# Windowed attention and a token and channel mixer on one core: the 64-row matmuls of token mixing replaced by 128-row ones

## The chip, the cores and the metric

The kernel runs on one core of a Trainium2 chip. A core has a matmul engine (PE; its weight loads are shown apart as PEld), a vector engine (DVE), an activation engine (ACT), a general engine (POOL) and a queue engine (SP) that issues transfers. Each takes its own instructions in order; they wait for each other through semaphores. The metric is the device time of one execution in microseconds, as the median of several runs; lower is better.

## The reference

Attention with a causal window of 64 positions over q, k, v of 8 batches, 8 heads, 576 positions and 64 elements per head; then a mixer over the 576 positions (tokens) and one over the 512 channels, each with a residual:

```python
scores = np.where((rel >= 0) & (rel < 64), q @ k.T / 8, -1e9)
x = softmax(scores) @ v                          # (8, 576, 512), heads side by side
h = relu(x.transpose(0, 2, 1) @ w_tok1) @ w_tok2 # w_tok1 576 x 256, w_tok2 256 x 576
u = x + h.transpose(0, 2, 1)
out = u + relu(u @ w_ch1) @ w_ch2                # w_ch1 512 x 1536, w_ch2 1536 x 512
```

All tensors are float32; the weights arrive as float64 and are converted on the chip.

## The kernel before, in words

The 576 positions of a batch are nine blocks of 64. A tile of 128 rows holds two blocks. Two batches (a pair) make nine tiles: four of the one batch, then a shared tile (`i % 9 == 4`) with the ninth block of the first batch in its top 64 rows and that of the second in its bottom 64 rows, then four of the other batch. There are 36 tiles, and one iteration of the main loop (lines 451 to 523) for each, in a software pipeline. In iteration `i` PE computes the scores of tile `i + 1` (`qk`, L257), transposes the first half of tile `i`'s exponentials (L292, copied out of PSUM by ACT at L294), runs a first piece of token mixing (line 486), transposes the second half, runs the first token product of tile `i - 1` (`tok1`, L348), multiplies the probabilities of tile `i` with v (`av`, L304) and runs a second piece (line 510). DVE masks the scores and takes their maximum (L274, L277), ACT takes the exponentials (L285), DVE normalizes (L318), ACT and POOL split the result into a rounded and a remainder part, xhi and xlo (L91, L94; for the shared tile L329 and L330). Between these DVE converts the float64 weights (L179 to L194), with the last addition on POOL (L196).

Products that need full precision are made of three: high by high, high by low, low by high. For the shared tile `split_x` puts the high part of one batch's block and its low part on top of each other in 128 rows (xhi for the first batch, xlo for the second), and the weights' rows of the ninth block are held twice, so that one 128-row matmul with t1hi makes two of the three products. The third, with t1lo, takes the 64 rows of the high part alone:

```python
x = xhi if rows is top else xlo
combos = ((t1hi, x, full), (t1lo, x, rows))
```

`tok1_part` is called four times with 64 rows in each pair's two iterations after the shared tile: two token halves for the first batch (top), two for the second (bottom), so 16 such matmuls in all.

A piece of token mixing (`tok2`) is one batch, one half of its positions and one group of 128 channels: it transposes x into PSUM (L383), adds six matmuls with the second token weights (L390), and ACT copies the result to u (L395). A piece of the first half has two transposes and 256 columns; one of the second half has a third transpose of 64 columns, from 64 rows of the shared tile, and 320 columns. There are 32 pieces of either kind. A table of counts (`PIECES`) sets how many run where: mostly one at line 486 and one at line 510, with the last ones after the loop.

The order of the instructions on each engine is that of the program. From line 572 on, the channel mixing runs on chunks of 512 tokens (L582, L618).

Of the kernel before, what the change touches and what calls it, by code (L numbers as in the profile page):

```python
# [10 lines left out]
F32 = mybir.dt.float32  # L11
F32R = mybir.dt.float32r
# [10 lines left out]
P = 128  # L23
BLK = 64
NBLK = S // BLK
NPAIR = B // 2
TPP = 9
NT = NPAIR * TPP
DT = 256
# [45 lines left out]
def mixer_kernel(ctx: ExitStack, tc: tile.TileContext, qh, kh, vh, wt1, wt2, wc1, wc2, out):  # L75
    nc = tc.nc
# [6 lines left out]
    ident = const.tile([P, P], F32, name="ident")  # L83
# [5 lines left out]
    def split(eng_hi, eng_lo, hi, lo, src):  # L89
        if eng_hi is nc.scalar:  # L90
            nc.scalar.copy(hi, src)  # L91
        else:
            eng_hi.tensor_copy(hi, src)
        eng_lo.tensor_sub(lo, src, hi.bitcast(F32))  # L94
# [18 lines left out]
    with ExitStack() as actx:  # L113
        pa = actx.enter_context(tc.tile_pool(name="pa", bufs=1))
# [24 lines left out]

        maskr = [pa.tile([P, P], F32R, name=f"maskr{m}") for m in range(2)]  # L140
        identr = pa.tile([P, P], F32R, name="identr")
        make_identity(nc, ident)
        nc.scalar.copy(identr, ident)
        for m in (1, 0):
            nc.gpsimd.memset(mask[m], 0.0)
            for half in range(2):
                mh = mask[m][half * BLK:(half + 1) * BLK]
                nc.gpsimd.affine_select(out=mh, in_=mh, compare_op=ALU.is_ge, fill=NEG,
                                        base=-1, pattern=[[1, P]], channel_multiplier=-1)
                nc.gpsimd.affine_select(out=mh, in_=mh, compare_op=ALU.is_ge, fill=NEG,  # L150
                                        base=BLK, pattern=[[-1, P]], channel_multiplier=1)
            if m == 1:
                nc.gpsimd.memset(mask[1][0:BLK, 0:BLK], NEG)
            nc.scalar.activation(maskr[m], mask[m], AF.Copy, scale=NEG_PE / NEG)

        t1hi = pa.tile([P, 5 * DT], F32R, name="t1hi")
        t1lo = pa.tile([P, 5 * DT], F32R, name="t1lo")
        t2hi = pa.tile([P, NTT * S], F32R, name="t2hi")
# [69 lines left out]
        def job_finish():  # L228
            if to_finish:
                n, w = to_finish.pop(0)  # L230
                finished.add(n)
                src, hi, lo, o, m = jobs[n]
                if hi is None:
                    nc.sync.dma_start(w2_dram[:, o:o + m], w)
                else:
                    eng = nc.vector if src is wt2 or n >= N_FIRST else nc.gpsimd
                    split(nc.scalar, eng, hi[:, o:o + m], lo[:, o:o + m], w)

        s_ps, e_sb, st = {}, {}, {}

# [56 lines left out]
        xs, xhl = {}, {}  # L297
# [23 lines left out]
        full, top, bottom = slice(0, P), slice(0, BLK), slice(BLK, P)  # L321
# [13 lines left out]
        h_ps = {}  # L335

        def tok1_part(i, b, rows, slot, first, last):
            xhi, xlo = xhl[i]
            if first:
                h_ps[b] = [ps.tile([P, C], F32, name=f"h{b}_{tt}", tag="h") for tt in range(NTT)]  # L340
            for tt in range(NTT):
                if rows is full:
                    combos = ((t1hi, xhi, full), (t1hi, xlo, full), (t1lo, xhi, full))
                else:
                    x = xhi if rows is top else xlo
                    combos = ((t1hi, x, full), (t1lo, x, rows))
                for n, (w, x, r) in enumerate(combos):
                    nc.tensor.matmul(h_ps[b][tt], w[r, slot * DT + tt * P:slot * DT + (tt + 1) * P], x[r],  # L348
                                     start=first and n == 0, stop=last and n == len(combos) - 1)

        pieces, up_tags = [], [("up", 1)]
# [18 lines left out]
        def tok2(b, half, ct, hh):  # L370
            assert len(finished) >= 7
            p, odd = divmod(b, 2)
            base = p * TPP + (5 if odd else 0)
            s0, n = (0, 256) if half == 0 else (256, 320)
            up = ps.tile([P, 512], F32, name=f"up{b}_{half}_{ct}", tag=up_tags[0][0], bufs=up_tags[0][1])
            up_tags.append(up_tags.pop(0))
            cs = slice(ct * P, (ct + 1) * P)
            segs = [(base + 2 * half + j, slice(0, P), j * P, P) for j in range(2)]
            if half == 1:
                r = slice(BLK, P) if odd else slice(0, BLK)  # L380
                segs.append((p * TPP + 4, r, 256, BLK))
            for j, (i, rows, o, m) in enumerate(segs):
                nc.tensor.matmul(up[:, o:o + m], xs[i][rows, cs], ident[rows, rows],  # L383
                                 start=(j == 0), stop=False, is_transpose=True, skip_group_check=True)
            k = 0
            for tt in range(NTT):
                hi, lo = hh[tt]
                for hx, w in ((hi, t2hi), (hi, t2lo), (lo, t2hi)):
                    k += 1
                    nc.tensor.matmul(up[:, :n], hx[:, cs], w[:, tt * S + s0:tt * S + s0 + n],  # L390
                                     start=False, stop=(k == 6), skip_group_check=True)
            if ct == 0:
                ust[b, half] = pa.tile([P, NCT, 320], F32, name=f"u{b}_{half}", tag="ust", bufs=2)
            us = ust[b, half]
            nc.scalar.copy(us[:, ct, :n], up[:, :n])  # L395
            if ct == NCT - 1:
                stores.append((us, b * S + s0, n))
                if b >= B - 2:
                    store_u()
# [3 lines left out]
        def store_u():  # L403
            while stores:
                us, g0, n = stores.pop(0)
                a = 0
                while a < n:
                    j, o = divmod(g0 + a, CHUNK)
                    m = min(n - a, CHUNK - o)
                    (nc.sync if g0 < (B - 1) * S - 320 else nc.scalar).dma_start(u_dram[j][:, :, o:o + m], us[:, :, a:a + m])  # L410
                    a += m

        def tok1(i):
            p, t = divmod(i, TPP)
            b0, b1 = 2 * p, 2 * p + 1
            if t < 4:
                tok1_part(i, b0, full, t, t == 0, False)
            elif t == 4:
                tok1_part(i, b0, top, 4, False, True)
                finish_h(b0)  # L420
            else:
                if t == 5:
                    tok1_part(i - 1, b1, bottom, 4, True, False)
                tok1_part(i, b1, full, t - 5, False, t == 8)
                if t == 8:
                    finish_h(b1)

        def run_pieces(k):
            for _ in range(min(k, len(pieces))):
                tok2(*pieces.pop(0))  # L430
# [15 lines left out]
        tok1_plan, n = {}, 0  # L446
        for i in range(TOK1_FROM, NT + 1):
            m = min(n + (1 if i < TOK1_SLOW else 2), i)
            tok1_plan[i] = range(n, m)
            n = m  # L450
        for i in range(-1, NT + 1):
# [26 lines left out]
            while to_finish:  # L478
                job_finish()
# [36 lines left out]
            if i == NT - 1:  # L516
                while to_convert or to_convert_b or to_finish:
                    job_convert_a()
                    job_convert_b()
                    job_finish()  # L520
                qctx.close()
                pu = uctx.enter_context(tc.tile_pool(name="pu", bufs=1, side="right", reuse_waits="tile"))
                ul = {0: load_u(0, pu)}
# [4 lines left out]
    with ExitStack() as bctx:  # L528
# [28 lines left out]
        def late_steps():  # L557

            job_abs()
            yield  # L560
            while to_convert or to_convert_b or to_finish:
                job_convert_a()
                if to_load:
                    job_load()
                yield
                job_finish()
                yield
                job_convert_b()
                job_abs()
                yield  # L570
# [89 lines left out]
```

## Time and profile before

| | |
|---|---|
| median of 3 runs | 886.76 us (886.35 to 886.89) |
| the profiled execution's own time | 888.41 us |
| its span in the profile | 886.5 us |
| PE busy | 864.6 us of the span |
| DVE, ACT, POOL busy | 372.3, 311.8, 101.4 us |
| token mixing and attention | to about 294 us, channel mixing from there |

PE is nearly always busy in the records, but the records of its matmuls overlap: what a matmul costs is read from the start of one to the start of the next. A row of the timeline gives the start, the duration, the engine, the line, and the operation with its output, inputs and shape, and, in square brackets, idle time ahead of it with the engine that ended it. Rows of the chain of work give start, duration, engine, output and line. Rows of groups give the count after the x, then the busy time in all and the mean duration in nanoseconds, then the idle time ahead. Rows of stretches of time give for each engine busy time and count, in the order PE, PEld, DVE, ACT, POOL, and then the granted PE clock as a share of full speed.

### The profile page before, as it was taken

What the parts mean: (1) busy time and instruction counts of PE and PEld (TensorE: products, weight loads), DVE (VectorE), ACT (ScalarE), POOL (GpSimd) and SP (SyncE); (2) the same over time, 40 slices, a digit from 0 to 9 for tenths busy, and PEclk for the clock granted to TensorE, in tenths of its full rate; (3) what the DMA queues carried; (4) which work ended last, traced back from release to release, by engine and by line L of the source; (5) the groups of instructions that cost most, each with busy time, mean ns of one, the idle gap of its engine ahead of it and who ended that gap; (6) DMA issues with size and microseconds to landing.
All of it is one profiled execution on the core that took longest, in us unless ns stands there. A gap on an engine that the chain in (4) does not pass through costs nothing.

```text
span 886.5 us, 14562 instructions
## 1 busy us (share of the span) xinstructions
PE 864.6 (98%) x6002; PEld 708.6 (80%) x6002; DVE 372.3 (42%) x701; ACT 311.8 (35%) x966; POOL 101.4 (11%) x104
## 2 busy tenths in 40 slices
PE   7899999999999999999999999999999999999998
PEld 4667878778768888888888888888888888888887
DVE  4978777787776598130220220230220220220211
ACT  4878778778776452120120120120120220220200
POOL 2433343333332000000000000000000000000000
PEclk9989999999999999999999999999999999999999
DMA  9557566566554442100100100100100100100001
GB/s 324 188 180 248 180 229 229 196 204 225 199 175 132 130 156 90 59 1 36 60 0 36 60 1 36 60 1 36 60 12 24 60 13 24 60 13 36 0 13 36
DMA packets 39906, 84.69 MB, mean 96 GB/s; under 512 B 5280, under 2 KB 18336, under 8 KB 37920
## 3 DMA queue, kind: packets, MB, share of 16 engines
q1 hardware_dynamic: 37728, 81.93, 27.5%
q10 hardware_dynamic: 2112, 1.84, 0.6%
q8 instruction: 47, 0.77, 0.4%
q14 instruction: 19, 0.16, 0.1%
HBM read 64.09 MB, written 19.66 MB: 94 GB/s over the span
## 4 chain that ended last, share of the span: by engine, by line
PE 84%; DVE 9%; ACT 4%; issue 1%; DMA 1%; SPq 0%; POOL 0%; DVEq 0%; ACTq 0%
PE op L618 33%; PE gp L582 31%; PE up L390 5%; PE xp L304 4%; PE s L257 4%; PE h L348 3%; PE up L383 2%; ACT e L285 2%; PE pp L292 2%; DVE nm L277 1%; DVE e L274 1%; ACT pt L294 1%; DMA k<-kh 1%; DVE r L194 1%; DVE c L191 1%
## 5 line engine op out<-in xcount | busy, mean ns | idle before, releaser
L586 ACT ACTIVATE ghi<-gp 128x512 fp32r<-128x512 f32 x108 | 64.6, 598 | 440.3 <-PE gp L582 439.9
L618 PE MATMUL op<-ghi,w2lo 128*128 128x512 f32 (+1 forms) x444 | 170.3, 384 | 0.2 <-DVE w2lo L94 0.2
L618 PE MATMUL op<-ghi,w2hi 128*128 128x512 f32 (+1 forms) x444 | 170.2, 383 | 0.0
L618 PE MATMUL op<-glo,w2hi 128*128 128x512 f32 (+1 forms) x444 | 170.2, 383 | 0.0
L582 PE MATMUL gp<-uhi,w1hi 128*128 128x512 f32 x432 | 168.1, 389 | 0.0
L582 PE MATMUL gp<-ulo,w1hi 128*128 128x512 f32 x432 | 168.1, 389 | 0.0
L582 PE MATMUL gp<-uhi,w1lo 128*128 128x512 f32 x432 | 168.1, 389 | 0.0
L587 DVE SCALAR_TENSOR_TENSOR glo<-gp,ghi 128x512 fp32r<-128x512 f32 x108 | 74.6, 691 | 190.6 <-ACT ghi L586 190.6
L620 DVE TENSOR_TENSOR uf<-op,uf 128x512 f32<-128x512 f32 (+1 forms) x37 | 25.0, 677 | 242.1 <-PE op L618 242.1
L618 PEld LDWEIGHTS op<-ghi,w2lo 128*128 128x128 f32 x444 | 83.5, 188 | 17.0 <-DVE w2lo L94 0.6
L618 PEld LDWEIGHTS op<-glo,w2hi 128*128 128x128 f32 x444 | 83.5, 188 | 16.4
L618 PEld LDWEIGHTS op<-ghi,w2hi 128*128 128x128 f32 x444 | 83.5, 188 | 16.3
L285 ACT ACTIVATE e<-e,nm 128x128 f32<-128x128 f32 x232 | 90.4, 393 | 13.9 <-DVE nm L277 11.4
L582 PEld LDWEIGHTS gp<-uhi,w1lo 128*128 128x128 f32 x432 | 81.1, 188 | 16.9
L582 PEld LDWEIGHTS gp<-ulo,w1hi 128*128 128x128 f32 x432 | 81.1, 188 | 16.8
L582 PEld LDWEIGHTS gp<-uhi,w1hi 128*128 128x128 f32 x432 | 81.1, 188 | 16.8
L304 PEld LDWEIGHTS xp<-v,pt 128*64 128x64 f32 x1152 | 41.0, 143 | 21.6 <-ACT pt L294 9.5
L304 PE MATMUL xp<-v,pt 128*64 128x64 f32 x1152 | 48.7, 234 | 6.4 <-ACT pt L294 6.0
L274 DVE SCALAR_TENSOR_TENSOR e<-s,mask 128x512 f32<-128x512 f32 x58 | 39.5, 680 | 26.7 <-PE s L257 26.7
L294 ACT COPY pt<-pp 128x512 f32<-128x512 f32 x72 | 41.7, 584 | 22.1 <-PE pp L292 21.7
L94 POOL TENSOR_TENSOR xlo<-x,xhi 128x512 fp32r<-128x512 f32 x32 | 41.2, 1287 | 55.5 <-ACT xhi L91 55.3
L257 PE MATMUL s<-k,q 64*64 64x128 f32 x1152 | 45.8, 295 | 1.4 <-DMA k<-kh 0.7
(72 smaller groups left out, 1000.0 us busy)
## 6 DMA issues: line engine op xcount, KB each, us to landing
v<-vh SPq DMA_DIRECT2D x36, 512.0 KB, 3.7
raw<-wc SPq DMA_DIRECT2D x32, 384.0 KB, 4.4
q<-qh SPq DMA_DIRECT2D x36, 256.0 KB, 4.1
k<-kh SPq DMA_DIRECT2D x7, 1280.0 KB, 7.8
out<-uf SPq DMA_DIRECT2D x35, 256.0 KB, 2.3
uf<-u_dram SPq DMA_DIRECT2D x8, 1024.0 KB, 5.8
u_dram<-u SPq DMA_DIRECT2D x7, 512.0 KB, 4.5
k<-kh SPq DMA_DIRECT2D x5, 256.0 KB, 7.0
```

Source lines behind the costliest of these rows:

```text
L94: eng_lo.tensor_sub(lo, src, hi.bitcast(F32))
L257: nc.tensor.matmul(s[u][half * BLK:(half + 1) * BLK, j], qt[r, j, half], kbs[b][r, j, n * BLK:n * BLK + P], start=not on_pe, stop=True, sk ...
L274: nc.vector.scalar_tensor_tensor(out=e, in0=s_ps.pop((i, u)), scalar=scale, in1=mk.unsqueeze(1).to_broadcast([P, 4, P]), op0=ALU.mult, op1 ...
L285: nc.scalar.activation(e[:, h], src[:, h], AF.Exp, bias=nm[:, g:g + 1], scale=by, accum_out=sm[:, g:g + 1])
L294: nc.scalar.copy(pt, pp)
L304: nc.tensor.matmul(xp[half * BLK:(half + 1) * BLK, h], pts[h % 2][:, h // 2, half * BLK:(half + 1) * BLK], vt[:, half, h], start=True, sto ...
L348: nc.tensor.matmul(h_ps[b][tt], w[r, slot * DT + tt * P:slot * DT + (tt + 1) * P], x[r], start=first and n == 0, stop=last and n == len(co ...
L390: nc.tensor.matmul(up[:, :n], hx[:, cs], w[:, tt * S + s0:tt * S + s0 + n], start=False, stop=(k == 6), skip_group_check=True)
L582: nc.tensor.matmul(gp, w[:, ct * F + ft * P:ct * F + (ft + 1) * P], x[:, ct], start=(k == 0), stop=(k == 3 * NCT - 1))
L586: nc.scalar.activation(ghi, gp, AF.Relu)
L587: nc.vector.scalar_tensor_tensor(out=glo, in0=gp, scalar=0.0, in1=ghi.bitcast(F32), op0=ALU.max, op1=ALU.subtract)
L618: nc.tensor.matmul(op, w[:, ct, ft], x[:, cols], start=(k == 0), stop=(k == 3 * NFT - 1))
```

## The change

Two kinds of 64-row work on PE become 128-row work, with zeros or a permutation in place of the narrower operand. For the third product of the shared tile a new tile `t1z` holds the low weights of the ninth block twice: once with the top 64 rows and zeros below, once with the bottom 64 rows and zeros above. POOL clears it at the start and copies the rows in when the last part of t1lo is done. For the third transpose the whole 128 rows of the shared tile are transposed, to 128 columns of PSUM of which 64 are used; for the second batch of a pair the identity has its two column halves swapped (`swapped`, made by two copies on POOL), so that the wanted block lands first. The two new tiles take 2.5 KB of each partition.

```diff
+        swapped = pa.tile([P, P], F32, name="swapped")
         make_identity(nc, ident)
...
+        for c in range(2):
+            nc.gpsimd.tensor_copy(swapped[:, c * BLK:(c + 1) * BLK], ident[:, (1 - c) * BLK:(2 - c) * BLK])
+
+        t1z = pa.tile([P, 2, DT], F32R, name="t1z")
+        nc.gpsimd.memset(t1z.bitcast(F32), 0.0)
...
                     split(nc.scalar, eng, hi[:, o:o + m], lo[:, o:o + m], w)
+                    if src is wt1 and o + m == 5 * DT:
+                        for c, r in enumerate((top, bottom)):
+                            nc.gpsimd.tensor_copy(t1z[r, c], t1lo[r, 4 * DT:].bitcast(F32))
...
-                    combos = ((t1hi, x, full), (t1lo, x, rows))
-                for n, (w, x, r) in enumerate(combos):
-                    nc.tensor.matmul(h_ps[b][tt], w[r, slot * DT + tt * P:slot * DT + (tt + 1) * P], x[r],
+                    combos = ((t1hi, x), (None, x))
+                for n, (w, x) in enumerate(combos):
+                    w, o = (t1z[:, rows is bottom], 0) if w is None else (w, slot * DT)
+                    nc.tensor.matmul(h_ps[b][tt], w[:, o + tt * P:o + (tt + 1) * P], x,
...
-            segs = [(base + 2 * half + j, slice(0, P), j * P, P) for j in range(2)]
+            segs = [(base + 2 * half + j, ident, j * P) for j in range(2)]
             if half == 1:
-                r = slice(BLK, P) if odd else slice(0, BLK)
-                segs.append((p * TPP + 4, r, 256, BLK))
-            for j, (i, rows, o, m) in enumerate(segs):
-                nc.tensor.matmul(up[:, o:o + m], xs[i][rows, cs], ident[rows, rows],
+
+                segs.append((p * TPP + 4, swapped if odd else ident, 256))
+            for j, (i, perm, o) in enumerate(segs):
+                nc.tensor.matmul(up[:, o:o + P], xs[i][:, cs], perm,
```

On PE, a piece of the second half of batch 1, the second of a pair, reads before like this; the shapes are those of the output, and the numbers behind the names tell buffers apart:

```order
L383 MATMUL up_1_0_1643<-ident,x_998 128x128
L383 MATMUL up_1_0_1643<-ident,x_1116 128x128
L383 MATMUL up_1_0_1643<-ident,x_689 128x64
L390 MATMUL up_1_0_1643<-t2hi,hhi_0_1208 128x320
L390 MATMUL up_1_0_1643<-t2lo,hhi_0_1208 128x320
```

And now:

```order
L393 MATMUL up_1_0_1650<-ident,x_1005 128x128
L393 MATMUL up_1_0_1650<-ident,x_1123 128x128
L393 MATMUL up_1_0_1650<-swapped,x_696 128x128
L400 MATMUL up_1_0_1650<-t2hi,hhi_0_1215 128x320
L400 MATMUL up_1_0_1650<-t2lo,hhi_0_1215 128x320
```

Nothing moved; the third transpose reads all rows of the shared tile against the swapped identity and writes 128 columns in place of 64.

On PE, the shared tile's first token product for batch 0, between the transposes of the exponentials and the attention product, before:

```order
L292 MATMUL pp_1_750<-ident,e_1_647 128x128 x4
L348 MATMUL h_0_448<-xhi_691,t1hi 128x512
L348 MATMUL h_0_448<-xhi_691,t1lo 128x512
L348 MATMUL h_1_449<-xhi_691,t1hi 128x512
L348 MATMUL h_1_449<-xhi_691,t1lo 128x512
L304 MATMUL xp_782<-v_485,pt_0_730 64x64 x2
```

And now:

```order
L301 MATMUL pp_1_757<-ident,e_1_654 128x128 x4
L358 MATMUL h_0_453<-xhi_698,t1hi 128x512
L358 MATMUL h_0_453<-xhi_698,t1z 128x512
L358 MATMUL h_1_454<-xhi_698,t1hi 128x512
L358 MATMUL h_1_454<-xhi_698,t1z 128x512
L313 MATMUL xp_789<-v_490,pt_0_737 64x64 x2
```

The order is the same; the matmuls that took 64 rows of t1lo take 128 rows of t1z.

On POOL, around the last part of t1lo (w is a converted piece of weights, xlo the remainder of a split tile), before:

```order
L94 TENSOR_TENSOR xlo_434<-x_426,xhi_433 128x512
L196 TENSOR_TENSOR w_461<-r_460,c_444 128x320
L94 TENSOR_TENSOR t1lo<-w_461,t1hi 128x320
L94 TENSOR_TENSOR xlo_536<-x_528,xhi_535 128x512
L196 TENSOR_TENSOR w_561<-r_560,c_546 128x384
```

And now:

```order
L94 TENSOR_TENSOR xlo_439<-x_431,xhi_438 128x512
L202 TENSOR_TENSOR w_466<-r_465,c_449 128x320
L94 TENSOR_TENSOR t1lo<-w_466,t1hi 128x320
L246 CAST t1z<-t1lo 64x256 x2
L94 TENSOR_TENSOR xlo_543<-x_533,xhi_542 128x512
L202 TENSOR_TENSOR w_568<-r_567,c_553 128x384
```

Two casts stand between t1lo and the split that followed it at once. Two copies into swapped and the memset of t1z stand behind the masks at the start of the same queue. On SP the order is unchanged, but the first of three late weight loads now waits for DVE as well as PE, which the second did before.

More of the change, by code (lines that the diff above doesn't have):

```diff
@@ L342, in tok1_part @@
                 if rows is full:
-                    combos = ((t1hi, xhi, full), (t1hi, xlo, full), (t1lo, xhi, full))
+                    combos = ((t1hi, xhi), (t1hi, xlo), (t1lo, xhi))
                 else:
                     x = xhi if rows is top else xlo
-                    combos = ((t1hi, x, full), (t1lo, x, rows))
-                for n, (w, x, r) in enumerate(combos):
-                    nc.tensor.matmul(h_ps[b][tt], w[r, slot * DT + tt * P:slot * DT + (tt + 1) * P], x[r],
+                    combos = ((t1hi, x), (None, x))
+                for n, (w, x) in enumerate(combos):
+                    w, o = (t1z[:, rows is bottom], 0) if w is None else (w, slot * DT)
+                    nc.tensor.matmul(h_ps[b][tt], w[:, o + tt * P:o + (tt + 1) * P], x,
                                      start=first and n == 0, stop=last and n == len(combos) - 1)
```

## The prediction

> **What bounds the kernel now.** I read the page first, then the chain of work that ended last.
>
> ```profile
> PE 864.6 (98%) x6002; PEld 708.6 (80%) x6002; DVE 372.3 (42%) x701; ACT 311.8 (35%) x966; POOL 101.4 (11%) x104
> PE 84%; DVE 9%; ACT 4%; issue 1%; DMA 1%; SPq 0%; POOL 0%; DVEq 0%; ACTq 0%
> ```
>
> PE carries 84% of the chain, so shorter PE work should count; but DVE and ACT hold 13%, and the changed lines run in the first 300 us, where these two are on the chain. There each place must be asked for itself: does PE set the pace, or does it wait behind the saved time?
>
> What 64-row work costs is read from the starts of the matmuls in the timeline of PE, since their durations overlap. First two pieces of token mixing near the end of the stage, one with two transposes and six 256-column matmuls, one with a third, 64-row transpose and six 320-column matmuls:
>
> ```profile
> 287.56 0.38 PE L383 MATMUL up<-ident,x 128*128 128x128 f32 x2
> ...
> 287.89 0.28 PE L390 MATMUL up<-t2lo,hhi 128*128 128x256 f32 x1
> ...
> 288.37 0.28 PE L390 MATMUL up<-t2hi,hlo 128*128 128x256 f32 x1
> 288.49 0.58 PE L383 MATMUL up<-ident,x 128*128 128x128 f32 x3
> ...
> 289.25 0.31 PE L390 MATMUL up<-t2lo,hhi 128*128 128x320 f32 x1
> ...
> 289.83 0.31 PE L390 MATMUL up<-t2hi,hlo 128*128 128x320 f32 x1
> 289.98 0.38 PE L383 MATMUL up<-ident,x 128*128 128x128 f32 x2
> ```
>
> The first piece takes 288.49 - 287.56 = 0.93, the second 289.98 - 288.49 = 1.49. A 256-column matmul steps by (288.37 - 287.89)/4 = 0.12, a 320-column one by (289.83 - 289.25)/4 = 0.145. Six of the first kind leave 0.93 - 0.72 = 0.21 for two transposes, 0.105 each. A piece with three whole transposes should take 0.93 + 0.105 + 6 x 0.028 = 1.21. So the 64-row transpose costs 1.49 - 1.21 = 0.28 more than a whole one: PE pauses on entering and on leaving the 64-row form.
>
> Then the shared tile in the first token product:
>
> ```profile
> L348 PE MATMUL h<-xlo,t1lo 64*128 64x512 f32 x8 | 4.0, 495 | 0.0
> ```
>
> ```profile
> 260.64 0.49 PE L348 MATMUL h<-xlo,t1lo 64*128 64x512 f32 x1
> 261.07 0.50 PE L348 MATMUL h<-xlo,t1hi 128*128 128x512 f32 x1
> ...
> 263.14 0.51 PE L348 MATMUL h<-xlo,t1hi 128*128 128x512 f32 x1 [0.71 <-POOL xlo L94]
> 263.48 0.40 PE L348 MATMUL h<-xhi,t1lo 128*128 128x512 f32 x1
> 263.71 0.40 PE L348 MATMUL h<-xhi,t1hi 128*128 128x512 f32 x1
> ```
>
> Where 64 and 128 rows alternate, a step takes 0.43 (261.07 - 260.64); between whole matmuls 0.23 (263.71 - 263.48). Each switch costs 0.20, a group of four up to 0.8. The row at 263.14 already warns: after this group PE stood waiting for POOL.
>
> [...]
>
> **The change part by part.**
>
> *32 transposes.* They fall in three places. Twelve lie in the first piece of an iteration (line 486), ahead of the second softmax transpose. They save PE 0.28 each, and the path nothing, as the ninth iteration shows (ACT, then PE), and the last of the twelve alike:
>
> ```profile
> 81.28 0.58 ACT L294 COPY pt<-pp 128x512 f32<-128x512 f32 x1
> ```
>
> ```profile
> 81.68 1.26 PE L304 MATMUL xp<-v,pt 128*64 128x64 f32 x32
> 82.88 0.64 PE L383 MATMUL up<-ident,x 128*128 128x128 f32 x3
> ...
> 84.52 0.44 PE L257 MATMUL s<-k,q 64*64 64x128 f32 x7
> ...
> 248.81 1.25 PE L304 MATMUL xp<-v,pt 128*64 128x64 f32 x32
> 249.99 0.33 PE L383 MATMUL up<-ident,x 128*128 128x128 f32 x1
> ```
>
> The attention product takes 82.88 - 81.68 = 1.20 (249.99 - 248.81 = 1.18 in the last), where an unhindered one takes 1.08 (rows at 61.35 and 62.43, below). The difference is a wait for the second pt copy, which ends at 81.86 behind four exponentials and a copy of u on ACT. That queue is fed from the scores and the first pt copy, both ahead of the piece. PE arrives 0.28 earlier and waits 0.28 longer: 0.
>
> Twelve lie in the second piece (line 510), behind the attention product and ahead of the next scores.
>
> ```profile
> 75.66 0.44 PE L383 MATMUL up<-ident,x 128*128 128x128 f32 x2
> ...
> 76.73 0.34 PE L257 MATMUL s<-k,q 64*64 64x128 f32 x4
> ```
>
> ```profile
> 85.66 0.69 DVE L274 SCALAR_TENSOR_TENSOR e<-s,mask 128x512 f32<-128x512 f32 x1 [1.39 <-PE s L257]
> ```
>
> This piece takes 84.52 - 82.88 = 1.64 now and should take 1.07 (76.73 - 75.66) + 0.105 + 0.17 = 1.35, so 0.29 less. Here DVE is waiting for the scores (1.39 idle), so the whole next iteration comes forward. One of the twelve runs into the block of the next paragraph; 11 x 0.29 = 3.2. The last eight, with no softmax behind them, go on PE without a gap: 8 x 0.28 = 2.2. Late next there is only the copy of u, on an ACT that has little else.
>
> *16 matmuls of the shared tile.* Four pairs of iterations hold them. Three pairs save nothing, since DVE holds the path from the first iteration into the second; the chain between 184 and 197:
>
> ```profile
> 184.18 0.70 DVE e L274
> ...
> 192.57 0.61 DVE x L318
> ...
> 197.06 0.45 PE xp L304 x7
> ```
>
> PE waits for the softmax of the next tile, its normalization and the pt copy. Its shorter groups only lengthen that wait. The first pair differs:
>
> ```profile
> 58.48 0.49 PE L348 MATMUL h<-xlo,t1lo 64*128 64x512 f32 x1
> ...
> 59.76 0.50 PE L348 MATMUL h<-xhi,t1hi 128*128 128x512 f32 x1
> ...
> 61.35 1.15 PE L304 MATMUL xp<-v,pt 128*64 128x64 f32 x32
> 62.43 0.34 PE L257 MATMUL s<-k,q 64*64 64x128 f32 x4
> ```
>
> ```profile
> 59.88 0.57 ACT L294 COPY pt<-pp 128x512 f32<-128x512 f32 x1
> ```
>
> The pt copy ends at 60.45, 0.90 before the product at 61.35. Three steps take 59.76 - 58.48 = 1.28 and will take 0.70; the step ahead of them holds one more switch, 0.20. Saved 0.78, all within the 0.90 of slack.
>
> *POOL.* Two copies for the swapped identity and one memset come behind the masks, where POOL idles until the first weights: 0. The two casts into t1z stand between the last t1lo and the split of xlo:
>
> ```profile
> L150 POOL TENSOR_SCALAR_AFFINE_SELECT mask<-mask 64x128 f32<-64x128 f32 x4 | 1.2, 290 | 0.3
> L145 POOL MEMSET mask<- 128x128 f32 x2 | 0.4, 202 | 0.0
> ```
>
> ```profile
> 35.23 0.87 POOL L94 TENSOR_TENSOR t1lo<-w,t1hi 128x320 fp32r<-128x320 f32 x1 [0.57 <-ACT t1hi L91]
> 36.06 1.27 POOL L94 TENSOR_TENSOR xlo<-x,xhi 128x512 fp32r<-128x512 f32 x1
> ```
>
> ```profile
> 36.19 1.16 DVE L272 TENSOR_SCALAR nm<-nm 128x4 f32<-128x4 f32 x1
> 37.65 0.36 DVE L181 TENSOR_SCALAR c<-c 128x384 f32<-128x384 f32 x1
> ```
>
> xlo itself has time. But DVE's tensor_scalar with four elements takes 1.16 because it starts inside POOL's instruction and ends with it (36.06 + 1.27 = 37.33). So DVE, on the path here, pays: nm will end with the first cast, the next conversion step with the second, and L181 with xlo, some 0.2 behind. With a cast of d, L181 ends near 37.69 + 2d, against 38.01 now: a loss of 2d - 0.32. For 256 columns d is 0.32 by the memset (0.9 ns a column and 0.09), 0.73 by the two-input rows (2.1 ns and 0.20), 0.49 by the affine select, the nearest, since it too reads one operand. Loss 0.3 to 1.1; I take 0.66.
>
> *Buffers.* 2.5 KB more in each partition shifts what later tiles overlay; one load of late weights waits for DVE too. It is read only in the channel stage, as the first conversion of late weights, and has some ten microseconds: 0. A first step of that conversion waits in addition for the last store of u, which overlays its tile; DVE has a gap behind it. DVE holds the chain for a stretch of the first chunk, too, but starts there on the results of PE's own first matmuls, and so shifts with them.
>
> Sum: 3.2 + 2.2 + 0.8 - 0.7 = 5.5 us off. The profiled execution took 888.41 itself and would take 882.9; the median of the runs, 1.65 lower, becomes 886.76 - 5.5 = 881.2.
>
> **The rivals.**
>
> Half clock (slower). After the waits of the shared tile the granted clock can fall:
>
> ```profile
> 184.60:188.00 3.40, 2.62 (x14) 1.26 (x11) 3.30 (x6) 3.28 (x13) 3.17 (x3) 1.00 0.76 264
> 188.00:191.40 3.40, 3.38 (x60) 3.16 (x60) 3.33 (x7) 2.39 (x9) 0.00 (x0) 0.51 1.01 319
> ```
>
> PE was busy for 2.62 of 3.40 and the next 3.40 ran at 0.51. The shorter groups lengthen just these waits. One such stretch over PE-bound work costs up to 1.7; it costs nothing where DVE holds the path, as here. One or two new ones after the third and fourth pair give 883 to 884.6; four on the path (6.8) take back more than is saved, and five (8.5) give 889.7, slower. For it: the waits grow by up to 0.8 in 3.4. Against: most of them lie ahead of DVE-bound work. [...]
>
> The first pieces count too. If ACT's queue came forward with PE, 12 x 0.28 = 3.4 more: 877.8. Against it stands the wait already seen at 81.68.
>
> The second pieces don't count. If the gain after each were taken up by DVE's conversions in the next iteration, 3.2 go: 884.4. Against it: 1.39 idle at 85.66.
>
> The switch doesn't vanish, because the neighbours have other forms (attention products use 128x64 and 64x64 tiles). Then only the POOL loss stays: 887.4. Against it: both pieces at 287.56 and 288.49 have whole neighbours.
>
> Half the rows are half the work (slower). If a 64-row step cost half of a whole one, widening would add 0.12 to each of 16 matmuls and 0.05 to each of 32 transposes: 886.76 + 3.5 = 890.3. [...] Against it: 0.43 beside 0.23.
>
> **How the numbers follow.** My forecast 0.66, one or two half-clock stretches 0.11, first pieces too 0.05, second pieces not 0.08, four stretches 0.01, five 0.03, a switch that stays 0.05, half work 0.01. The forecast's own range is 880.3 (POOL 0.3, and 0.02 to 0.05 more a piece) to 882.5 (POOL 1.1, a tenth lost at some of the places); the range over the cases is 879.4 to 884.5. This kernel's measurement tells about 0.2%, 1.8 us: faster means below 885.0, slower above 888.5. The first four cases are faster, 0.90; four stretches and the switch that stays are the same, 0.06; five stretches and half work are slower, 0.04.
>
> **What would show it.** PE: the pieces at the stage's end 1.21 apart, steps of 0.23 throughout the shared groups. The twelve attention products behind a first piece with 320 columns: 1.45 instead of 1.20. The second token stage starts some 5.5 earlier, and all after it is shifted, not shortened. DVE near 38: L181 behind xlo. I am wrong if the products stay at 1.20 (then ACT moved), if PE's clock shows new stretches of 0.5 before 300, or if L257 follows the second pieces no sooner.

## The result and the profile after

The changed kernel took 882.38 us in the median of four runs (881.58 to 883.42), against 886.83 for the kernel before beside it: a ratio of 0.995 (95% interval 0.9936 to 0.9963), 4.5 us faster. The forecast was 881.2, its range 879.4 to 884.5. The profiled execution took 883.42 itself and has a span of 881.6. Line numbers of an experiment can stand a few lines off. Lines of the changed kernel that answer to those of before: pieces L393 and L400 (before L383, L390), first token product L358 (L348), attention product L313 (L304), scores L266 (L257), pt copy L303 (L294), channel mixing L592 and L628 (L582, L618), late conversion on ACT L175 (L169).

The busy times of the page, and the chain of work that ended last, by engine:

```profile
PE 849.2 (96%) x6002; PEld 702.9 (80%) x6002; DVE 372.4 (42%) x701; ACT 310.8 (35%) x966; POOL 103.4 (12%) x109
PE 76%; DVE 12%; ACT 8%; issue 2%; DMA 1%; POOL 0%; POOLq 0%; SPq 0%; DVEq 0%; ACTq 0%
```

PE lost 15.4 us of busy time with the same number of instructions (some of it by the granted clock, see below), and the span lost 4.9. The chain moved from PE (84% before) to DVE and ACT: much of what PE saved was not on the path.

The pieces at the end of the token stage, in the timeline of PE:

```profile
282.71 0.38 PE L393 MATMUL up<-ident,x 128*128 128x128 f32 x2
282.93 0.27 PE L393 MATMUL up<-swapped,x 128*128 128x128 f32 x1
...
283.91 0.38 PE L393 MATMUL up<-ident,x 128*128 128x128 f32 x2
...
286.31 0.39 PE L592 MATMUL gp<-uhi,w1hi 128*128 128x512 f32 x1
```

A piece takes 283.91 - 282.71 = 1.20, where it took 1.49. The pieces with a scores group behind them moved the stage by 0.28 to 0.29 each, eleven times. The attention product behind a first piece, in the same view:

```profile
78.47 0.34 PE L313 MATMUL xp<-v,pt 128*64 128x64 f32 x4
78.98 1.03 PE L313 MATMUL xp<-v,pt 128*64 128x64 f32 x28 [0.17 <-ACT pt L303]
79.95 0.55 PE L393 MATMUL up<-ident,x 128*128 128x128 f32 x3
```

It now takes 79.95 - 78.47 = 1.48 instead of 1.20, and its gap is put down to ACT's pt copy. Eleven of the twelve show 1.45 to 1.49, and these pieces gained nothing. The twelfth, in the second pair's shared block, shows 2.08: there the shortened group of the shared tile lies ahead of the same wait too, and that gain is lost as well.

The shared tile's group in the first pair:

```profile
55.53 0.39 PE L358 MATMUL h<-xlo,t1z 128*128 128x512 f32 x1
55.77 0.40 PE L358 MATMUL h<-xlo,t1hi 128*128 128x512 f32 x1
56.00 0.39 PE L358 MATMUL h<-xlo,t1z 128*128 128x512 f32 x1
56.23 0.40 PE L358 MATMUL h<-xhi,t1hi 128*128 128x512 f32 x1
```

Steps of 0.23 in place of 0.43.

The second token stage ended, and the first chunk of channel mixing began, at 286.31 instead of 294.46: 8.15 earlier. Of this some 2.4 are the granted clock and none of the change's: the clock's first record at full speed is at 17.5 us instead of 20.8 (32 scores matmuls there take 1.10 instead of 1.71), where no changed matmul runs yet, worth 1.25, and the stretch at half clock that the profile of before has from 51.5 to 58.3 is missing (the repeat below, whose mean clock is 0.996 where it is 0.998 here, has it again), worth 1.1 more. What is left, 5.8, is the size of the forecast. But the end of the kernel came only 4.9 earlier, so 3.3 were given back, all in one place: the first chunk's second product (L628, from its first matmul to the next chunk's first) took 36.38 instead of 33.11. Every chunk behind it takes what it took. The chain at that place:

```profile
286.51 0.44 ACT u L405
286.97 7.13 DMA u_dram<-u
294.13 0.56 ACT c L175
```

ACT's first step of the late conversion waits until the last store of u has landed, because its output now lies where that u lay. It starts 294.13 - 286.31 = 7.81 behind the start of the stage; before, 297.89 - 294.46 = 3.43. ACT idles for 4.21 ahead of this step, and the activation behind it (L596) starts at 294.58, though PE's last matmul for that one (from 291.55, 0.39 long) had ended at 291.94. DVE's conversion gets its input from ACT, and PE in the end needs the converted weights (timeline of PE, then two stretches of 3.41 us: span, then busy time and count of PE, PEld, DVE, ACT and POOL, granted clock, DMA):

```profile
326.85 0.50 PE L628 MATMUL op<-ghi,w2lo 128*128 128x512 f32 x1 [1.81 <-DVE w2lo L94]
```

```profile
324.71:328.12 3.41, 1.60 (x8) 1.05 (x7) 3.31 (x8) 0.96 (x2) 0.00 (x0) 1.00 0.39 112
328.12:331.53 3.41, 3.41 (x10) 2.65 (x9) 3.27 (x8) 0.92 (x2) 0.00 (x0) 0.50 0.16 23
```

PE stands for 1.81 us, 0.18 before, and the stretch behind that wait runs at half clock (0.50), which takes the other 1.6. So two theories went to the chip. A: the new layout of the pool costs this, since the last store is late. B: the layout is harmless and the 3.3 us are an accident of the clock.

### The profile page after: what moved, and what is told of

Its sections match the earlier page's. It is cut to its first block, busy times and chain, and to the rows that moved or that the text cites. A ratio compares the mean times of both kernels' runs of the same rounds, so it can differ in the third digit from the quotient of the medians.

```text
span 881.6 us, 14566 instructions
## 1 busy us (share of the span) xinstructions
PE 849.2 (96%) x6002; PEld 702.9 (80%) x6002; DVE 372.4 (42%) x701; ACT 310.8 (35%) x966; POOL 103.4 (12%) x109
## 4 chain that ended last, share of the span: by engine, by line
PE 76%; DVE 12%; ACT 8%; issue 2%; DMA 1%; POOL 0%; POOLq 0%; SPq 0%; DVEq 0%; ACTq 0%
PE op L628 33%; PE gp L592 30%; ACT e L294 4%; PE s L266 4%; PE xp L313 3%; PE up L400 3%; ACT pt L303 2%; DVE nm L286 2%; DVE e L283 2%; PE up L393 1%; DVE r L200 1%; DVE c L187 1%; DMA u_dram<-u 1%; ACT u L405 1%; DVE c L197 1%
## 5 line engine op out<-in xcount | busy, mean ns | idle before, releaser
L596 ACT ACTIVATE ghi<-gp 128x512 fp32r<-128x512 f32 x108 | 64.5, 597 | 432.3 <-PE gp L592 431.9
L628 PE MATMUL op<-ghi,w2lo 128*128 128x512 f32 (+1 forms) x444 | 171.0, 385 | 1.8 <-DVE w2lo L94 1.8
L628 PE MATMUL op<-glo,w2hi 128*128 128x512 f32 (+1 forms) x444 | 170.9, 385 | 0.0
L628 PE MATMUL op<-ghi,w2hi 128*128 128x512 f32 (+1 forms) x444 | 170.7, 384 | 0.0
L592 PE MATMUL gp<-ulo,w1hi 128*128 128x512 f32 x432 | 168.1, 389 | 0.0
L592 PE MATMUL gp<-uhi,w1hi 128*128 128x512 f32 x432 | 168.1, 389 | 0.0
L592 PE MATMUL gp<-uhi,w1lo 128*128 128x512 f32 x432 | 168.0, 389 | 0.0
L628 PEld LDWEIGHTS op<-ghi,w2lo 128*128 128x128 f32 x444 | 83.8, 189 | 18.7 <-DVE w2lo L94 2.2
L628 PEld LDWEIGHTS op<-ghi,w2hi 128*128 128x128 f32 x444 | 83.9, 189 | 16.5
L628 PEld LDWEIGHTS op<-glo,w2hi 128*128 128x128 f32 x444 | 83.7, 189 | 16.6
L294 ACT ACTIVATE e<-e,nm 128x128 f32<-128x128 f32 x232 | 90.4, 393 | 14.7 <-DVE nm L286 12.2
L592 PEld LDWEIGHTS gp<-uhi,w1lo 128*128 128x128 f32 x432 | 81.1, 188 | 16.9
L592 PEld LDWEIGHTS gp<-uhi,w1hi 128*128 128x128 f32 x432 | 81.1, 188 | 16.8
L592 PEld LDWEIGHTS gp<-ulo,w1hi 128*128 128x128 f32 x432 | 81.1, 188 | 16.8
L313 PEld LDWEIGHTS xp<-v,pt 128*64 128x64 f32 x1152 | 39.6, 139 | 27.9 <-ACT pt L303 15.3
L313 PE MATMUL xp<-v,pt 128*64 128x64 f32 x1152 | 48.7, 229 | 10.8 <-ACT pt L303 9.9
L303 ACT COPY pt<-pp 128x512 f32<-128x512 f32 x72 | 41.7, 584 | 18.8 <-PE pp L301 18.4
L266 PE MATMUL s<-k,q 64*64 64x128 f32 x1152 | 43.1, 284 | 2.7 <-DVE c L197 1.6
```

The costliest lines, as they stand in the source:

```text
L266: nc.tensor.matmul(s[u][half * BLK:(half + 1) * BLK, j], qt[r, j, half], kbs[b][r, j, n * BLK:n * BLK + P], start=not on_pe, stop=True, sk ...
L294: nc.scalar.activation(e[:, h], src[:, h], AF.Exp, bias=nm[:, g:g + 1], scale=by, accum_out=sm[:, g:g + 1])
L303: nc.scalar.copy(pt, pp)
L313: nc.tensor.matmul(xp[half * BLK:(half + 1) * BLK, h], pts[h % 2][:, h // 2, half * BLK:(half + 1) * BLK], vt[:, half, h], start=True, sto ...
L592: nc.tensor.matmul(gp, w[:, ct * F + ft * P:ct * F + (ft + 1) * P], x[:, ct], start=(k == 0), stop=(k == 3 * NCT - 1))
L596: nc.scalar.activation(ghi, gp, AF.Relu)
```

## The experiments

### Layout and change, one without the other

Both parts of the change, with the two new tiles where they move nothing:

```diff
-        swapped = pa.tile([P, P], F32, name="swapped")
+        swapped = const.tile([P, P], F32, name="swapped")
-        t1z = pa.tile([P, 2, DT], F32R, name="t1z")
+        t1z = pq.tile([P, 2, DT], F32R, name="t1z")     # behind the first loads
```

> Both parts of the change, but the new tiles take no room in the pool of the token stage: the swapped identity is allocated with the constants, the low weights with zero rows in the pool of q, k and v, whose space the first load of u takes over. The tile of the late conversion then overlays what it overlaid before, and every wait on ScalarE, SyncE and (but for one) VectorE is the one it was before. Theory A (the moved overlay gives back 1.8 us of the gain, 3.3 with the half-clock stretch that follows): 880.3 to 881.3 us, 5.6 to 6.4 below the kernel before; the last store of u is no longer what the first late step on ScalarE waits for, and chunk 0's group of op lasts 33.1 us as in the profile of before. Rival B (the layout is harmless, the 36.4 us of that group came from the granted clock alone): 882.4, as the changed kernel, and the group lasts as long as there.

880.96 us; ratio to before 0.9935 (0.9923 to 0.9947), 5.7 us faster. The store as the transfers' view has it, and PE's wait:

```profile
u_dram<-u ACTq DMA_DIRECT2D x1, 640.0 KB, 3.5
```

```profile
324.96 0.50 PE L628 MATMUL op<-ghi,w2lo 128*128 128x512 f32 x1 [0.16 <-DVE w2lo L94]
```

The wait is back to 0.16 and the group to 33.10. The opposite arm, the kernel before with an unused tile:

```diff
         identr = pa.tile([P, P], F32R, name="identr")
+        pa.tile([P, 640], F32, name="shift_a")
```

> The kernel before with one unused tile of 2.5 KB per partition at the place of the swapped identity, so that all that lies behind it in the pool moves up as in the changed kernel. No instruction is added. Theory A: 1.8 us slower than before (888.6), up to 3.3 where the half clock follows (890.1); the first late step on ScalarE waits for the last store of u. Rival B: as before, 886.8 within 0.5.

887.21 us; ratio 1.0006 (0.9996 to 1.0016). Theory A had the place right and the price wrong. In the chain the wait stands where it said, with a shorter store:

```profile
294.57 6.09 DMA u_dram<-u
300.68 0.56 ACT c L170
```

PE waits 0.76 there and the group takes 33.70: 0.6 more, not 1.8, within what the median can't tell from nothing. Then the changed kernel once more:

> The changed kernel once more, beside the others on one chip, and with a second profile. Theory A (the moved overlay costs what the last store of u is late): again above both parts with the old overlay (881.0), at 881.8 to 882.6; in the profile the first late step on ScalarE again starts 6.5 us or more behind the start of the channel stage, where it starts 3.4 behind with the old overlay, and chunk 0's group of op lasts 33.7 (a store of 6.1 us, as in the kernel before with the moved layout) to 36.4. Rival B (the difference was chance): 881.0 within 0.5, and the group lasts 33.1.

883.33 us; ratio 0.9966 (0.9953 to 0.9979), which lies above that of the old layout by 0.31% or 2.7 us, and the intervals don't meet. In this profile no half clock falls into the first chunk, and the group takes 34.76. So B falls, though the interval of the first comparison alone (0.9936 to 0.9963) does meet the old layout's; the 3.3 us of the first profile are 1.6 of waiting and 1.6 of clock. The medians put the layout at 2.7 (and at 2.2 in a later pair) where the traces show 1.6. The mean granted clock of each timed run is on record and accounts for most of the difference. At a mean clock of 0.998 the old layout took 880.89 to 881.36 and the changed kernel, in both its series, 882.32 to 883.94; at 1.0 it was 880.02 against 881.58 and 881.87. That is a layout worth 1.7 to 2.1 at equal clock. Three of the nine repeats ran at 0.994, and none of the five runs of the old layout did.

What sets the price shows when the runs stand side by side (the last two are told below). "Late" is how far the first late step on ACT starts behind the stage, "wait" PE's idle time before w2lo, "group" the first chunk's second product:

| kernel | layout | late | wait | group | median |
|---|---|---|---|---|---|
| before | old | 3.43 | 0.18 | 33.11 | 886.83 |
| before, unused tile | new | 6.76 | 0.76 | 33.70 | 887.21 |
| changed | new | 7.81 | 1.81 | 36.38 | 882.38 |
| changed again | new | 7.82 | 1.82 | 34.76 | 883.33 |
| changed, store in parts | new | 7.34 | 1.34 | 34.29 | 881.70 |
| changed, old layout | old | 3.44 | 0.16 | 33.10 | 880.96 |
| changed, copy ahead | new | 7.75 | 1.75 | 34.70 | 876.09 |
| the same, old layout | old | 3.44 | 0.16 | 33.10 | 873.90 |

In every row of the new layout the wait is the lateness less 6.00: 6.76 - 0.76, 7.81 - 1.81, 7.34 - 1.34, 7.75 - 1.75. The slack is the same in all, 6.00 - 3.43 = 2.6 behind the old start, and each tenth beyond it is paid in full. By these numbers a store of 3.5 us, issued 0.66 behind the start of the stage, would have landed at 4.2 and cost nothing; this is an estimate.

### Why the store is late

In the old layout the three loads of the first late weights are issued 10.8 to 5.1 us ahead of the stage and are over by then. In the new one all three go out from 0.9 ahead of it to 0.7 behind, beside the store. The added wait for DVE is not the one that ends last: in the trace of the changed kernel the first load goes out at 285.63, released by the end of the last piece's transposes on PE (L393). These are the transfers of the changed kernel around 287; the last number is the time from issue to landing:

```profile
raw<-wc SPq DMA_DIRECT2D x2, 384.0 KB, 5.8
u_dram<-u ACTq DMA_DIRECT2D x1, 640.0 KB, 7.1
```

The store takes 3.5 alone and 6.1 to 7.1 beside the loads, though the loads are on SP's queue and the store on ACT's. The pair of the kernel before with and without the unused tile shows it with nothing else changed (6.1 and 3.5); no run held back the loads alone.

If size were what holds it up, a small last part would land sooner:

```diff
+            if b == B - 1 and half == 1:
+                j, o = divmod(b * S + s0, CHUNK)
+                nc.scalar.dma_start(u_dram[j][:, ct:ct + 1, o:o + n], us[:, ct:ct + 1, :n])
-            if ct == NCT - 1:
+            elif ct == NCT - 1:
```

> The changed kernel with its own layout, but the last u is stored in four parts, each behind its own copy, in place of one store of 640 KB behind the fourth. The first late step still waits for them. If it is the lateness of that store that costs, and the last part of 160 KB lands sooner (some 4 us after its issue in place of 7.1), that step starts some 3 us earlier against the channel stage (4.8 behind its start in place of 7.8), chunk 0's group of op lasts 33.1 to 33.6 and the time is 881.0 to 881.6, against 882.4 to 883.3. If three loads beside it hold up the small part as long as the large one: no change, 882.4 to 883.3.

881.70 us; ratio 0.9941 (0.9927 to 0.9956). By the median this could be either, since it overlaps the changed kernel. The chain decides:

```profile
287.81 6.13 DMA u_dram<-u
...
293.95 0.55 ACT c L175
```

The last 160 KB took 6.13 us, and the late step starts 0.47 earlier, not 3. A quarter of the bytes took nearly as long beside the same three loads. The part ahead of it, issued 0.98 earlier, was in flight too, so the run doesn't part the loads from the store's own earlier parts; it shows that the size of the last transfer is not what sets its time.

### The two parts apart

The transposes alone (the old layout from here on, unless said):

> The shared tile transposed whole with the swapped identity, which lies with the constants; the steps of 64 rows on the low weights stay. Old overlay. By the sum of the prediction: 3.2 from eleven second pieces and 2.0 from the last eight (2.2 less the wait that the trace after shows), 5.2 in all: 881.6 us. If half a microsecond or more hid elsewhere (the twelve first pieces gain too), 878 to 879; if the transposes were worth nothing outside the last eight, 884.6.

881.78 us; ratio 0.9942 (0.9927 to 0.9956), 5.1 faster, where 5.2 were expected. The zero rows alone:

> The low weights with zero rows alone, in the pool of q, k and v; the transposes stay as before. Old overlay. By the sum: 0.78 gained in the first pair's shared group, 0.26 (measured in the changed kernel; 0.66 forecast) lost to the two casts, so 0.5 faster, 886.3. If the other three pairs gain what their steps get shorter, 0.59 each, 884.5. If the casts cost more than the groups give, 887.

887.62 us; ratio 1.0002 (0.9991 to 1.0013): nothing that can be told from no change, and an expected gain of 0.5 can't be either. Its trace is clearer. Against the profile of before, PE is 1.42 ahead when it comes to the token product behind the casts and 1.15 ahead after it: 0.27 lost. Across the first pair's shared groups, where both profiles have a stretch at half clock, the lead grows from 1.15 to 1.83: 0.7 gained. The second and fourth pair leave it as it was, within 0.1. In the third it falls by 1.1, and the stretches show what differs:

```profile
190.57:193.98 3.41, 1.84 (x7) 0.97 (x7) 3.34 (x7) 2.68 (x10) 3.00 (x3) 1.00 0.70 279
193.98:197.39 3.41, 3.41 (x38) 2.55 (x37) 0.96 (x3) 2.67 (x12) 0.26 (x1) 0.50 0.02 5
```

A half-clock stretch that lay at 188.0 before, under DVE's path, lies here on PE's own work behind the shared group. That is the forecast's rival of the half clock, seen in one profile of one kernel, and the likely cause there.

Then the transposes by their place. The code picks the whole or the 64-row form by a flag, set around the call at line 486 (the first pieces), or around everything else:

```diff
+            whole[0] = True      # the other way round in the second kernel
             run_pieces(min(have, n_pieces[0]))
+            whole[0] = False
```

> The shared tile transposed whole only where a piece runs as the first of its step (twelve pieces of 320 columns); the second pieces and the last eight keep their 64-row transposes, and the low weights stay. Old overlay. By the prediction (the attention product behind it waits as much longer as the piece is shorter): 0, so 886.7. Rival: each is worth what it is shorter, 12 x 0.29 = 3.5, so 883.2.

885.95 us; ratio 0.9994 (0.9985 to 1.0004): 0.5, with an interval from 1.3 faster to 0.4 slower, and far from 3.5. The kernel holds more than the text above says: three of the last eight pieces also run at line 486, in the last iterations, so fifteen transposes are whole. The trace parts them: PE's lead over the profile of before is 1.70 at 66 us and 1.74 at 270, behind all twelve, and grows by 0.55 in the last iterations. The twelve gave nothing, and the 0.5 is the size of the other three.

> The shared tile transposed whole in the second pieces and the last eight alone, the other half of the run before. Old overlay. By the prediction 3.2 + 2.0 = 5.2, so 881.5, the same as with all transposes whole (881.8). Rival: 3.5 less of the gain, 885.

881.79 us; ratio 0.9942 (0.9929 to 0.9955), which the medians can't tell from all transposes together. This kernel has twelve second pieces and five of the last eight whole, and its lead grows by 4.7 in the trace where that of all transposes whole grows by 5.3; the 0.6 between them is what the three late pieces gave in the run before. Twelve transposes, shorter by the same 0.28 each, are worth nothing at the first line; those at the second and at the end of the stage carry the whole gain.

### The copy that hides the first pieces

If the pt copy on ACT is what the attention product waits for, behind the exponentials and the piece's own copy of u, then the cover can be moved:

```diff
+            if 0 <= i < NT and not early:
+                pts.append(pt_transpose(i, 1))
             run_pieces(min(have, n_pieces[0]))
             have = min(have, len(pieces))
             if not early:
                 for _ in range(n_jobs):
                     job_convert_a()
-            if 0 <= i < NT and not early:
-                pts.append(pt_transpose(i, 1))
```

> Both parts with the old overlay (881.0), and in each step from the seventh on the second group of transposed probabilities, with ScalarE's copy of it (pt), stands ahead of the first piece instead of behind it. If that copy, behind the piece's own copy of u on ScalarE, is what makes the twelve products wait longer by what the piece got shorter, their 1.45 us go back to 1.20 or less: 12 x 0.28 = 3.4 or more gained, 877.6 or below. Rival: another wait ends there at the same time (ScalarE's exponentials, or the buffer of up), and the time stays at 881.0 within 0.5; or the piece's copy of u, now behind, holds up the second piece and it gets slower, 882 or more.

873.90 us; ratio 0.9858 (0.9844 to 0.9872): 12.6 us faster than before and some 7 faster than with the copy behind, twice what was expected. The same iteration, first as it was (both parts, old layout; ACT, then PE):

```profile
77.80 0.41 ACT L403 COPY u<-up 128x320 f32<-128x320 f32 x1
78.11 0.58 ACT L301 COPY pt<-pp 128x512 f32<-128x512 f32 x1
```

```profile
78.23 0.34 PE L311 MATMUL xp<-v,pt 128*64 128x64 f32 x4
78.74 1.03 PE L311 MATMUL xp<-v,pt 128*64 128x64 f32 x28 [0.17 <-ACT pt L301]
79.71 0.55 PE L391 MATMUL up<-ident,x 128*128 128x128 f32 x3
```

and with the copy ahead:

```profile
77.64 0.57 ACT L301 COPY pt<-pp 128x512 f32<-128x512 f32 x1
78.11 0.42 ACT L403 COPY u<-up 128x320 f32<-128x320 f32 x1
```

```profile
78.04 1.26 PE L311 MATMUL xp<-v,pt 128*64 128x64 f32 x32
79.23 0.55 PE L391 MATMUL up<-ident,x 128*128 128x128 f32 x3
```

The product takes 79.23 - 78.04 = 1.19 instead of 1.48. The waits between 65 and 275 us (engine and tile that waited, for whom: total, times, longest), with the copy behind, and ahead:

```profile
PE xp L311 <- ACT pt L301: 7.8, 21, 1.0
```

```profile
PE xp L311 <- ACT pt L301: 2.3, 3, 1.0
```

They fall by 5.5, and there were 21 of them, not twelve: pieces with 256 columns had a wait behind them too. Whether the move has a gain of its own, or also lets the first pieces count, was asked from both sides: the move on the kernel before, and the move on the changed one with 64-row transposes kept in the first pieces (the flag of above).

> The kernel before, with its 64-row work, but with ScalarE's copy of the second group of transposed probabilities ahead of the first piece. The move gained 7.0 us on both parts with the old overlay (873.9 against 881.0). Theory: with the copy ahead the twelve first pieces count in full, so the two parts are worth 5.7 + 3.5 = 9.2 here, and this kernel takes 883.1. Rival: the move has a gain of its own and the first pieces stay hidden behind another wait: 5.7, so 879.6.

883.06 us; ratio 0.9956 (0.9943 to 0.9968).

> The fastest kernel so far (873.9: both parts, old overlay, copy ahead of the piece), but the twelve first pieces keep their 64-row transposes. Theory: 12 x 0.29 = 3.5 slower, 877.4. Rival, as for the run before: first pieces hidden, 873.9 within 0.7.

878.16 us; ratio 0.9898 (0.9884 to 0.9913), 0.40% or 3.5 us above all pieces whole. Both go the theory's way and are far from the rivals: with the copy ahead the change is worth 883.06 - 873.90 = 9.2 in place of 5.7 (8.7 by the ratios to before, since the two medians are of different series). But the first pieces don't count in full, and the match with 3.5 is in part luck. The kernel with 64-row first pieces again has fifteen of them. By the traces the kernel with all pieces whole gains 2.35 on it over the twelve, 0.20 each, and 0.54 in the last iterations. The rest is lost to a wait that remains: the attention products behind the whole pieces mostly take 1.13 to 1.19, those behind the 64-row pieces 1.08. The move alone is worth 3.8; that was the half of the 7 not expected.

Last, the changed kernel in its own layout with the copy ahead:

> The changed kernel as it is, with its own layout, and the copy ahead of the piece. Theory A (the moved overlay costs what the last store of u is late): 1.6 to 2.7 above the same kernel with the old overlay, so 875.5 to 876.6, and chunk 0's group of op lasts 33.7 or more. Rival B: 873.9 within 0.5 and 33.1.

876.09 us; ratio 0.9883 (0.9867 to 0.9900), 2.2 above the old layout, with a wait of 1.75 for w2lo. The layout costs here what it costs in the changed kernel.

## Why the prediction was right, and where it was wrong

The time was right, within the range and on the side forecast, and most of the mechanism with it. How near it came is in part luck. The first series of the changed kernel ran at mean clocks of 0.998 and 1.0. The repeat, at 0.994 to 0.998, took 883.33 and was 3.0 faster than before, where 5.5 were forecast; that is still within the range over the cases, but beyond the forecast's own, which ended at 882.5. The terms one by one:

- **Second pieces, 3.2, and the last eight, 2.2.** Right: 0.28 to 0.29 each in the trace. The last eight lost 0.32 again where the token product of the last tile waits for its xlo (1.39 to 1.71 for six matmuls), so 5.1 in all, and 5.1 is what the transposes alone measured. The rival in which second pieces don't count is out.
- **First pieces, 0.** Right, and for the reason given: whole transposes there moved PE by less than 0.1 over the twelve, and by 2.35 once the pt copy stood ahead of the piece. The rival of 877.8 was for the most part a real gain with another order of two lines.
- **First pair's shared group, 0.78, the other three 0.** 0.7 in the trace of the zero rows alone, and nothing in the second and fourth pair; in the third a half-clock stretch hid what there was. The medians can't show terms of this size.
- **POOL's casts, a loss of 0.66.** The mechanism was right, the size not: 0.26 in the changed kernel, outside the 0.3 to 1.1 given. The working was also at odds with itself: it lets L181 end "some 0.2 behind" xlo, but 37.69 is the end of xlo, 37.33, and 0.36; with 0.2 the loss would have been 0.50. The timelines of POOL and DVE:

```profile
34.91 0.94 POOL L246 CAST t1z<-t1lo 64x256 fp32r<-64x256 f32 x2
35.92 1.28 POOL L94 TENSOR_TENSOR xlo<-x,xhi 128x512 fp32r<-128x512 f32 x1
```

```profile
36.09 1.32 DVE L188 TENSOR_SCALAR c<-c 128x384 int32<-128x384 int32 x1
37.45 0.56 DVE L197 SCALAR_TENSOR_TENSOR c<-raw,c 128x384 int32<-128x384 int32 x1
```

  The casts take 0.47 each, near the 0.49 taken. But the step supposed to end with xlo was L187 (L181 before); in their time DVE got one step further, and the one behind it, L188, runs for 1.32, to 37.41, just past the end of xlo at 37.20. The same step took 0.36 in the profile of before (L182, at 38.04), where POOL was idle. The step ahead of it shows the two lengths in that profile alone: L181 took 0.36 beside an idle POOL (at 37.65) and 1.06, to 73.76, where it started at 72.70 inside POOL's split of w1lo, which ended at 73.54.
- **Buffers, 0.** This is the step that failed. "A first step of that conversion waits in addition for the last store of u, which overlays its tile; DVE has a gap behind it": the wait was named and the cover was named, but neither had a length. The cover was 2.6 us, and the lateness 4.4. In the profile of before the store landed in 3.5, with nothing beside it; the forecast missed that the load which "waits for DVE too", priced at 0 for itself, goes out late, and that three loads then run beside the store. It cost 1.6, and 3.3 with the half clock behind. Without the new layout the kernel takes 880.96, 0.2 below the forecast, so the other terms came out near in sum; at a median clock of 0.998 against 0.996 before, that too is a little flattered.
- **The half clock.** In the profile of the changed kernel one new stretch came (0.50 from 328.12 to 331.53), but not behind the shared tile's groups: it came behind the wait for w2lo. The forecast looked for stretches before 300 only.
- **The switch that stays, and half work for half the rows.** Both out: steps of 0.23 where 0.43 stood, and whole transposes at 0.11. No run shows one of these 64-row steps at half the time of a whole one.

## What to carry to other kernels

A shorter instruction is worth its saving only where the next wait behind it isn't already set by another engine: find the copy or conversion the next group waits for, and ask whether the order of two lines could put it ahead, since that decided 0 or 2.4 us here and brought 3.8 more of its own. When a change adds a tile to a pool, list the waits that the shifted overlays add or move, and give each a length and each cover a length, in the company of the transfers that will be in flight then. Place a new tile so that nothing behind it moves, where there is room.

## What the runs showed of the hardware

- In these runs a store's time followed its company more than its size: 640 KB took 3.5 us alone and 6.1 to 7.1 beside three loads of 384 KB; 160 KB took 6.1 beside them and another part of 160 KB.
- The granted clock doesn't follow from PE's idle time alone. Behind a stretch with 1.60 us of 3.41 busy it fell to half (changed kernel, above); at the same place of the changed kernel with the copy ahead, 1.66 of 3.41 was followed by full clock:

```profile
317.82:321.23 3.41, 1.66 (x8) 1.07 (x7) 3.27 (x8) 0.99 (x3) 0.00 (x0) 1.00 0.34 88
321.23:324.65 3.42, 3.42 (x17) 2.81 (x16) 3.28 (x9) 0.62 (x2) 0.00 (x0) 1.00 0.21 51
```

What tells these two apart stays open. A single pair of profiles can therefore differ by 1 to 2 us in places that a change doesn't touch, as these do near 15 and 51 us, and terms below a microsecond are to be read from the place itself.
